# Attention of all four batches in halves of 256 queries with single-precision scores, in a fused attention and two-layer kernel

## The chip, the cores and the metric

One core of one Trainium2 chip. The metric is the device time of one execution in microseconds (us); less is better. The kernel before was run three times for its time, and one more execution was recorded by the hardware profiler.

## What is computed

Thresholded attention over 4 batches, 8 heads, 576 positions of 64 numbers, then two feed-forward layers over the 2304 rows that come out. All inputs are single precision.

```python
scores = scale * np.matmul(q, k.transpose(0, 1, 3, 2))       # 4, 8, 576, 576
thresh = np.max(scores, axis=-1, keepdims=True) - tau
scores = np.where(scores >= thresh, scores, -1000000000.0)
attn = np.exp(scores - np.max(scores, axis=-1, keepdims=True))
attn = attn / (np.sum(attn, axis=-1, keepdims=True) + 1e-09)
x = np.matmul(attn, v)                                       # to 2304 rows of 512
...
h = x @ w_in1; r = np.maximum(h, 0.0); x = (s * (r * r) + b) @ w_out1     # layer 1
h = x @ w_in2; x = (h * (1 / (1 + np.exp(-1.702 * h)))) @ w_out2          # layer 2
```

## The kernel before

**One planned order.** Every step is recorded with the engines it may run on, a cost and a due time (`Plan.add`). `Plan.run` then walks through the program once, always taking the ready step with the earliest due time, and writes out one fixed order for each engine. The due times come from the table `KN`. An engine executes its list strictly in order, so a step that has to wait holds up everything behind it on that engine.

**Attention** (`attention`, `heads`, `tile_step`). Two heads are handled together (`hp` 0 to 3), and the queries are cut in two parts: `w` = 0 holds queries 0 to 255, `w` = 1 queries 256 to 575. A pair (batch, `w`, `hp`) has four tiles of 128 queries (two per head), and with `w` = 1 a fifth that merges the last 64 queries of both heads. That makes 32 pairs and 144 tiles. For each tile TensorE writes scores into one of two buffers `S`; VectorE takes the negated row maximum `nm`; a bias `nb` and a bound `tb` are made from it; ScalarE takes the exponential `e`; and VectorE masks `e` by the bound, sums it, and with that lets go of `S`. For the units computed in half precision (all but the first two) ScalarE rounds `e` to `p16`, GpSimd computes the rest that the rounding left, a DMA transposes both into `PT`, and after the pair's last tile TensorE multiplies `PT` by V (the "mix").

`heads` decides the order of pairs by `KN["half"]`. Batches below it are "apart": all four head pairs of `w` = 0, then all four of `w` = 1, each with its own K and Q. With `half` = 2 this holds for batches 0 and 1. In batches 2 and 3 the two parts of a head pair follow each other and share K and Q (`"first"`).

The scores come in two forms, by `KN["parts"]` = 8. In batches 0 and 1 K is loaded as `kk` and scaled in place (L395), and single-precision products of 64 rows are used, each half of the array taking one half of the keys (L557). In batches 2 and 3 `prep_parts` cuts K and Q in two parts of reduced precision, one stacked above the other in 128 rows: ScalarE L411 and L419, VectorE L414 and L427, GpSimd L423 to clear borders. The scores are then four products of 128 rows per head and tile (L550).

**Layer 1** works on units of 256 rows: unit 2b + w needs the four pairs (b, w). `pair` makes the hidden values (L1035), `bank` the outputs (L1123). In `bank` one PSUM bank holds two halves of 256 columns. 48 products fill one half, ScalarE reads it with scale and bias (L1146), then 48 products fill the other half, which is read as well.

**Layer 2** works on blocks of 512 rows (`hidden7` L1333, `rows2` L1420).

**Engines.** TensorE, VectorE, ScalarE, GpSimd and SyncE, which issues every DMA, are PE, DVE, ACT, POOL and SP in the profile. A DMA whose buffer is not free yet holds up SP's whole queue.

Of the kernel before, what the change touches and what calls it, by code (L numbers as in the profile page):

```python
# [9 lines left out]
F32 = mybir.dt.float32  # L10
# [5 lines left out]
AF = mybir.ActivationFunctionType  # L16
ALU = mybir.AluOpType
# [4 lines left out]
P = 128  # L22
# [14 lines left out]
LOG_SP = 11.0 * math.log(2.0)  # L37
# [1 line left out]


KN = {
# [8 lines left out]
    "parts": 8, "raw": 1, "spread": 8,  # L50
}


# [219 lines left out]
def pe16(n, cols):  # L273
    return n * (cols * 0.4167 + 1.5)

def act(cols, psum=False):
    return cols * 0.834 + (53.0 if psum else 93.0)
# [12 lines left out]
class Kernel:  # L290
# [9 lines left out]
    def consts(self, pool):  # L300
        nc = self.nc
        self.ident = pool.tile([P, P], F32, name="ident")
        make_identity(nc, self.ident)
        self.ones = pool.tile([P, P], F32, name="ones")
        nc.vector.memset(self.ones, 1.0)
        self.turns, self.tw = 0, [Buf(None, "tw", None, None) for _ in range(KN["tw"])]
        for i, tw in enumerate(self.tw):
            tw.tile = pool.tile([P, 512, 2], F16, name="tw%d" % i)
            nc.vector.memset(tw.tile, 2.0 ** -24)
        sc = pool.tile([P, 3], F32, name="scal")  # L310
        for i, src in enumerate((self.tau, self.s, self.b)):
            nc.sync.dma_start(sc[:, i : i + 1], src.partition_broadcast(P))
        self.s_ap, self.b_ap = sc[:, 1:2], sc[:, 2:3]

        z = pool.tile([P, 1], F32, name="z")
        nc.vector.tensor_scalar(z, sc[:, 0:1], 0.0, None, ALU.is_ge)
        self.qs = pool.tile([P, 1], F32, name="qs")
        nc.vector.tensor_scalar(self.qs, z, 1.0 / math.sqrt(D), None, ALU.mult)
        t1 = pool.tile([P, 1], F32, name="t1")
        nc.vector.tensor_scalar(t1, z, -3e38, 3e38, ALU.mult, ALU.add)  # L320
        t2 = pool.tile([P, 1], F32, name="t2")
        nc.vector.tensor_scalar(t2, sc[:, 0:1], 0.0, None, ALU.max)
        self.under = pool.tile([P, 1], F32, name="under")
        nc.vector.tensor_tensor(self.under, t1, t2, ALU.add)


    def copy(self, dst, src, reads, writes, cols, scale=None, psum=False, also=0, **kw):
# [188 lines left out]
    def tile_step(self, p, i):  # L516


        nc, add = self.nc, self.plan.add
        k, q = p["k"], p["q"]  # L520
        Sp, swap = self.ps("S", [P, 2, 512]), []
        if not p["f32"] and p["unit"] * NP + p["hp"] < KN["sx"]:
# [3 lines left out]
            if self.nth % 3 == 0:  # L526
                Sp, swap = Buf(self.py, "Sx", [P, 2, 512], F32, 1), self.swaps
        T, q0 = p["T"], p["q0"]
        if i < 2 * T:
            h, t = divmod(i, T)  # L530
# [31 lines left out]
        else:  # L562
            used, cost = [k] + [q[h] for h, _ in heads], pe(1, HALF, True) + 200.0
        add({"PE": (cost, 60.0)}, scores, used + swap, [Sp])
        Sv = lambda: Sp[:, :, :HALF]
        nm = self.at("nm", [P, 1], F32, bufs=4)
        tb = self.at("tb", [P, 1], F32, bufs=4)
        pace, plain = p["pace"] / p["count"], p["f32"] and KN["nbs"]

        add(  # L570
            {"DVE": 668.0}, lambda _: nc.vector.tensor_reduce(nm.ap, Sv(), AX.XY, ALU.max, negate=True), [Sp], [nm],  # L571
            prio=self.plan.prio - KN["nm"] * pace,
        )
        add(
            {"POOL": 300.0} if p["f32"] and KN["tbp"] else {"DVE": 121.0},
            lambda e: self.eng[e].tensor_scalar(tb.ap, nm.ap, -1.0, self.under, ALU.mult, ALU.subtract), [nm], [tb],
            prio=self.plan.prio - KN["tb"] * pace,
        )
        nb = nm
        if not plain:  # L580
            nb = self.at("nb", [P, 1], F32, bufs=4)
            add(
                {"DVE": 65.0},
                lambda _: nc.vector.tensor_scalar(nb.ap, nm.ap, LOG_SP, None, ALU.add), [nm], [nb],  # L584
                prio=self.plan.prio - KN["tb"] * pace - 1.0,
            )
        e = self.at("e", [P, S], F32, bufs=KN["eb"])
        ev = lambda: e.ap.rearrange("p (a b) -> p a b", a=2)
        add(
            {"ACT": 624.0},  # L590
            lambda _: nc.scalar.activation(ev(), Sv(), AF.Exp, bias=nb.ap, scale=1.0), [Sp, nb], [e],  # L591
        )
        add(
            {"DVE": 735.0},
            lambda _: nc.vector.scalar_tensor_tensor(  # L595
                ev(), Sv(), tb.ap, ev(), ALU.is_ge, ALU.mult, accum_out=p["acc"][:, i, 0:1]
            ),
            [Sp, tb, e], [e, (p["acc"], i)], prio=self.plan.prio - KN["sc"] * pace,
        )
        if p["f32"]:  # L600
            Tp = Buf(self.px, "TP", [P, 2, 512], F32, 1)
# [290 lines left out]
    def gate(self, bank):  # L892

        return self.changes if bank.pool is self.pw else []
# [214 lines left out]
    def bank(self, u, ib):  # L1109

        nc, add, sv = self.nc, self.plan.add, self.scale_of(0)
        n = 256
        yp = self.bank_of([P, 2, n])
        ev = Buf(self.wp, "gt", [P, 2, n], F32, KN["gt"])
        terms = [(c, j, i, k) for c in range(NCH) for j in range(CH) for i, k in ((0, 0), (0, 1), (1, 0))]
        for h in range(2):
            i0 = 2 * ib + h
            m = KN["bn"]
            for part in range(0, 48, m):
                def mm(_, h=h, i0=i0, part=part):  # L1120
                    for t in range(part, part + m):
                        c, j, i, k = terms[t]
                        nc.tensor.matmul(  # L1123
                            yp[:, h, :], self.W[0, 1, c][:, i, j, i0 * P : (i0 + 1) * P], u["g"][c][:, k, j, :],
                            start=t == 0, stop=t == len(terms) - 1,
                        )
                c = part // 12
                add(
                    {"PE": (pe16(m, n), 60.0 * (part + m == 48))}, mm,
                    [self.W[0, 1, c], u["g"][c]] + self.gate(yp) + [(yp, 0)] * h, [(yp, h)],  # L1130
                )
            b = u["b"]
            if (ib, h) == (0, 0):
                ub = lambda: self.ub[:, b : b + 1]

                def scale(_):
                    if b == B:
                        nc.vector.tensor_reduce(ub(), self.ub[:, :B], AX.X, ALU.max)
                    y = sv["y"][:, b : b + 1]
                    nc.vector.tensor_scalar(y, ub(), ub(), sv["U"][:, 0:1], ALU.mult, ALU.mult)  # L1140
                    nc.vector.tensor_scalar(y, y, 2.0 ** 28, self.s_ap, ALU.mult, ALU.mult)
                if u["at"] == 0 or u["n"] == KN["fu"]:
                    add(self.tiny(2), scale, [sv["U"], (self.ub, b)], [(sv["y"], b)])
            add(
                {"ACT": act(n, True) + 190.0},
                lambda _, h=h, i0=i0: nc.scalar.activation(  # L1146
                    ev[:, h, :], yp[:, h, :], AF.Identity, bias=sv["b"][:, i0 : i0 + 1], scale=sv["y"][:, b : b + 1]
                ),
                [(yp, h), sv["b"], (sv["y"], b)], [(ev, h)],
            )  # L1150
        yd, cols = self.yd[u["b"]], slice(u["at"], u["at"] + n)
        self.load(
            lambda: yd[:, 2 * ib : 2 * ib + 2, cols], lambda: ev.ap, [(yd, (ib, u["at"]))], P * 2 * n * 4, reads=[ev]
        )
# [432 lines left out]
class Later:  # L1587


    pool = None  # L1590
# [50 lines left out]
```

## Time and profile before

| | us |
|---|---|
| median of 3 runs (lowest, highest) | 1044.27 (1041.58, 1047.13) |
| the profiled execution, its own time | 1043.83 |
| its span, first to last instruction | 1042.0 |
| TensorE busy | 986.9 |
| VectorE busy | 717.1 |
| ScalarE busy | 638.2 |
| GpSimd busy | 227.1 |

The profile is one execution on the hardware. Times inside it count from the start of the span. The granted clock is TensorE's, as a share of full speed. Idle time of an engine is put down to what ended it.

### The profile page before, as it was taken

To read this page: it belongs to the slowest core of one execution; us is meant where nothing else is said; L and a number is where in the kernel's file an instruction comes from. 1 tells how busy PE (TensorE), PEld (TensorE's weight loads), DVE (VectorE), ACT (ScalarE), POOL (GpSimd) and SP (SyncE) were. 2 spreads that over 40 slices of the span, in tenths; PEclk is the share of its full clock that TensorE was granted. 3 is DMA by queue.
4 is the path that set the end of the run, shared out by engine and by line. 5 is a ranking of instruction groups with operands and counts; after the bars stand their busy time and mean duration, and the time that the engine had idled before them with its cause. 6 is when DMAs were issued, how large, how long until landed. Compare 5 with 4: busy or idle time off the path is not lost.

```text
span 1042.0 us, 21397 instructions
## 1 busy us (share of the span) xinstructions
PE 986.9 (95%) x8181; PEld 747.5 (72%) x8181; DVE 717.1 (69%) x1670; ACT 638.2 (61%) x1220; POOL 227.1 (22%) x348
## 2 busy tenths in 40 slices
PE   5799989879999988999989999999999999999998
PEld 3466667658888876888868888887487487487483
DVE  6888897688888687987766867697257257256240
ACT  5787885588686675666755765685355355355241
POOL 1111134444544454444540000000001001000000
PEclk9999999899999998999989999999999999999999
DMA  7875589646678576566652336310010010000000
GB/s 250 279 268 168 161 170 222 130 89 152 127 163 184 127 155 127 130 129 136 147 102 84 114 112 214 120 51 3 31 51 2 31 50 2 31 31 1 31 11 20
DMA packets 170757, 114.80 MB, mean 110 GB/s; under 512 B 136280, under 2 KB 146592, under 8 KB 170656
## 3 DMA queue, kind: packets, MB, share of 16 engines
q1 hardware_dynamic: 170656, 113.45, 42.3%
q8 instruction: 64, 1.05, 0.4%
q14 instruction: 37, 0.30, 0.1%
HBM read 71.57 MB, written 10.00 MB: 78 GB/s over the span
## 4 chain that ended last, share of the span: by engine, by line
PE 53%; DVE 3%; DMA 3%; ACT 2%; issue 1%; POOL 0%; ACTq 0%; POOLq 0%; DVEq 0%
PE a L1420 18%; PE a L1333 8%; PE yy L1035 5%; PE y L1123 5%; PE yy L1123 4%; PE yy L1333 3%; PE y L1035 2%; PE d L1333 2%; PE S L550 2%; DMA PT<-p 2%; PE y L1333 2%; PE yy L1389 1%; PE T L690 1%; DMA wst<-in_moe_w_out 1%; PE y L1389 1%
## 5 line engine op out<-in xcount | busy, mean ns | idle before, releaser
L619 POOL TENSOR_TENSOR p<-e,p 128x512 f16<-128x512 f32 x108 | 129.9, 1203 | 187.5 <-ACT p L338 149.3
L1123 PEld LDWEIGHTS <-wb 128*128 128x128 f16 x1536 | 147.6, 98 | 26.5 <-issue 8.3
L1035 PEld LDWEIGHTS <-wb 128*128 128x128 f16 x1536 | 148.4, 98 | 25.1 <-issue 7.0
L1420 PE MATMUL a<-wb,g 128*128 128x512 f16 x648 | 144.4, 379 | 0.0
L1333 PEld LDWEIGHTS <-l 128*128 128x128 f16 x1344 | 131.5, 98 | 17.6
L595 DVE SCALAR_TENSOR_TENSOR e<-S,tb,e 128x576 f32<-128x576 f32 x144 | 116.0, 811 | 24.3 <-ACT e L591 21.9
L571 DVE TENSOR_REDUCE nm<-S 128x1 f32<-128x576 f32 x144 | 106.3, 750 | 36.1 <-PE S L557 19.4
L1420 PEld LDWEIGHTS <-g 128*128 128x128 f16 x648 | 63.4, 98 | 73.7
L1123 PE MATMUL yy<-g,wb 128*128 128x256 f16 x960 | 112.5, 273 | 2.6 <-ACT gt L1146 2.4
L591 ACT ACTIVATE e<-S,nb 128x576 f32<-128x576 f32 x108 | 78.8, 735 | 48.5 <-DVE nb L584 25.0
L1035 PE MATMUL yy<-xs,wb 128*128 128x256 f16 x912 | 107.5, 273 | 0.0
L1333 PE MATMUL a<-xs,l 128*128 128x256 f16 x768 | 95.6, 273 | 0.0
L338 ACT ACTIVATE p<-e 128x576 f16<-128x576 f32 x108 | 72.8, 677 | 24.9 <-DMA PT<-p 14.1
L1035 PE MATMUL y<-xs,wb 128*128 128x256 f16 x624 | 75.1, 273 | 4.5 <-ACT gt L1042 4.5
L340 ACT ACTIVATE gt<-a,x2y 128x512 f32<-128x512 f32 x18 | 12.4, 687 | 107.4 <-PE a L1420 84.3
L353 POOL TENSOR_TENSOR st<-wb 128x512 f32<-128x512 f32 x6 | 8.8, 1467 | 297.7 <-PE a L1333 171.6
L1123 PE MATMUL y<-g,wb 128*128 128x256 f16 x576 | 68.1, 273 | 2.0 <-ACT gt L1146 2.0
L1345 ACT ACTIVATE wb<-a 128x256 f32<-128x256 f32 x96 | 36.3, 378 | 33.0 <-PE a L1333 32.6
L1285 ACT ACTIVATE gt<-wb,x2h 128x256 f32<-128x256 f32 x64 | 36.5, 608 | 31.6 <-DVE wb L1352 31.6
L353 DVE TENSOR_TENSOR g<-gt,g 128x512 f16<-128x512 f32 x63 | 50.4, 801 | 7.6 <-ACT g L338 6.7
L550 PE MATMUL S<-kk,qb 128*128 128x288 f32 x160 | 41.2, 341 | 9.7 <-DVE nb L584 5.5
L1420 PE MATMUL a<-wb 128*128 128x512 f16 x216 | 49.4, 379 | 0.0
(194 smaller groups left out, 1749.6 us busy)
## 6 DMA issues: line engine op xcount, KB each, us to landing
wst<-in_moe_w_in SPq DMA_DIRECT2D x32, 512.0 KB, 5.4
wst<-in_moe_w_out SPq DMA_DIRECT2D x32, 512.0 KB, 4.1
rv<-in_v SPq DMA_DIRECT2D x32, 320.0 KB, 3.7
kk<-in_k SPq DMA_DIRECT2D x16, 288.0 KB, 4.6
raw<-in_k SPq DMA_DIRECT2D x16, 288.0 KB
yd<-gt SPq DMA_DIRECT2D x18, 256.0 KB, 2.5
raw<-in_q SPq DMA_DIRECT2D x16, 288.0 KB
wb<-yd SPq DMA_DIRECT2D x16, 256.0 KB, 4.3
```

The source lines that it names most:

```text
L338: nc.scalar.activation(dst(), src(), AF.Copy)
L353: engines, lambda e: self.eng[e].tensor_tensor(dst(), a(), b(), op), reads, writes, **kw
L550: nc.tensor.matmul(Sp[:, half, :HALF], q[h][j][:, qcols[h]], k[h][:, half * HALF : (half + 1) * HALF], start=(h, j) == (heads[0][0], 0), s ...
L571: {"DVE": 668.0}, lambda _: nc.vector.tensor_reduce(nm.ap, Sv(), AX.XY, ALU.max, negate=True), [Sp], [nm],
L591: lambda _: nc.scalar.activation(ev(), Sv(), AF.Exp, bias=nb.ap, scale=1.0), [Sp, nb], [e],
L595: lambda _: nc.vector.scalar_tensor_tensor(ev(), Sv(), tb.ap, ev(), ALU.is_ge, ALU.mult, accum_out=p["acc"][:, i, 0:1]),
L619: nc.gpsimd.tensor_tensor(p16[:, S + H2 :], e[:, :MAIN], p16[:, :MAIN], ALU.subtract)
L1035: nc.tensor.matmul(hps[:, h, :], W[:, i, j, kk * P : (kk + 1) * P], x[:, k, kk, :], start=t == 0, stop=t == len(terms) - 1,)
L1123: nc.tensor.matmul(yp[:, h, :], self.W[0, 1, c][:, i, j, i0 * P : (i0 + 1) * P], u["g"][c][:, k, j, :], start=t == 0, stop=t == len(terms) ...
L1285: lambda _, cols=cols, h=h: nc.scalar.activation(gt[:, cols], h(), AF.Tanh, scale=th[:, c : c + 1]),
L1333: nc.tensor.matmul(to(bank), W[:, u, m, j, kk * P : (kk + 1) * P], y[:, v, z, kk, :], start=n == 0 and not more, stop=n == 5, skip_group_c ...
L1420: nc.tensor.matmul(yp(), part(f, k), self.W[1, 1, f // CH][:, w, f % CH, :], start=n == 0, stop=n == 47,)
```

## The change

The diff, cut to its core. The table `KN` is replaced: the entries that select a form are shown, and nearly all due times in it have new values.

```diff
 KN = {
-    "first": 305.71, ... "half": 2, ... "t2": 670.54, "d2": 78.45, ... "tb": 54.91, ... "parts": 8,
+    "first": 278.77, ... "half": 4, "a2b": 247.09, "p2b": -5.0, "a3b": 450.05, "p3b": 4.03,
+    ... "t2": 642.87, "d2": 92.1, ... "tb": 13.38, ... "parts": 16,
 }
 # consts
+        self.signs, self.offs = pool.tile([P, 2], F32, name="signs"), pool.tile([P, 2], F32, name="offs")
+        nc.vector.memset(self.signs[:, 0:1], -1.0)
+        nc.vector.memset(self.signs[:, 1:2], 1.0)
+        nc.vector.tensor_scalar(self.offs[:, 0:1], self.under, -1.0, None, ALU.mult)
+        nc.vector.memset(self.offs[:, 1:2], LOG_SP)
 # tile_step
-        add(
-            {"POOL": 300.0} if p["f32"] and KN["tbp"] else {"DVE": 121.0},
-            lambda e: self.eng[e].tensor_scalar(tb.ap, nm.ap, -1.0, self.under, ALU.mult, ALU.subtract), [nm], [tb],
-        ...
-        if not plain:
-            add({"DVE": 65.0},
-                lambda _: nc.vector.tensor_scalar(nb.ap, nm.ap, LOG_SP, None, ALU.add), [nm], [nb], ...
+        both = self.at("tb", [P, 2], F32, bufs=4)
+        tb, nb = lambda: both[:, 0:1], lambda: both[:, 1:2]
+        if plain:
+            add({"POOL": 300.0},
+                lambda _: nc.gpsimd.tensor_scalar(tb(), nm.ap, -1.0, self.under, ALU.mult, ALU.subtract), [nm], [both], ...
+        else:
+            add({"DVE": 130.0},
+                lambda _: nc.vector.scalar_tensor_tensor(both.ap, self.signs, nm.ap, self.offs, ALU.mult, ALU.add), [nm], [both], ...
 # bank
                 if u["at"] == 0 or u["n"] == KN["fu"]:
                     add(self.tiny(2), scale, [sv["U"], (self.ub, b)], [(sv["y"], b)])
+        for h in range(2):
+            i0 = 2 * ib + h
             add(
                 {"ACT": act(n, True) + 190.0},
                 lambda _, h=h, i0=i0: nc.scalar.activation(
                     ev[:, h, :], yp[:, h, :], AF.Identity, bias=sv["b"][:, i0 : i0 + 1], scale=sv["y"][:, b : b + 1]
                 ),
-                [(yp, h), sv["b"], (sv["y"], b)], [(ev, h)],
+                [yp, sv["b"], (sv["y"], b)], [(ev, h)],
             )
```

So all four batches run "apart", `prep_parts` and the products of L550 are no longer used, one VectorE step writes bound and bias as two columns of one tile, and ScalarE reads a bank of layer 1 after both of its halves.

Counted over the whole program, VectorE has 128 instructions less (no `nb`, no L414 and L427), ScalarE 28, GpSimd 28; SP issues 16 DMAs more (16 more loads of `kk`, and 16 more each of `qa` and `qb`, against 32 loads of `raw` that go); TensorE has 160 products less, all of them scores. The new table also moves steps. Three places show how.

TensorE, the last pair of batch 3's attention (tiles 140 to 144 of 144), before; `S_7932` is the merged tile and the last two rows begin a mix:

```order
L550 MATMUL S_7887<-kk_7449,qb_7439 128x288 x2
L550 MATMUL S_7887<-kk_7449,qa_7437 128x288 x2
L550 MATMUL S_7907<-kk_7449,qb_7439 128x288 x2
L550 MATMUL S_7907<-kk_7449,qa_7437 128x288 x2
L638 MATMUL T_7919<-ident_71,ri_7912 4x128
L550 MATMUL S_7932<-kk_7449,qb_7439 128x288 x2
L550 MATMUL S_7932<-kk_7449,qa_7437 128x288 x2
L550 MATMUL S_7932<-kk_7699,qb_7557 128x288 x2
L550 MATMUL S_7932<-kk_7699,qa_7552 128x288 x2
L550 MATMUL S_7951<-kk_7699,qb_7557 128x288 x2
L690 LDWEIGHTS V_6334
L690 MATMUL T_7968<-PT0_7798,V_6334 64x256
```

Four of the five tiles stand behind each other with one small transpose among them, and no product of layer 1 stands between the first and the fifth.

The same engine and place in the changed kernel, from the second of the five tiles (`S_7361` is the merged one):

```order
L562 MATMUL S_7353<-kk_6917,qa_6860 128x288 x2
L562 MATMUL S_7361<-kk_6917,qa_6860 64x288 x2
L562 MATMUL S_7361<-kk_6917,qb_6927 64x288 x2
L644 MATMUL T_7368<-ident_71,ri_7356 5x128
L1129 LDWEIGHTS wb_2755
L1129 MATMUL y_7303<-g_7131,wb_2755 128x256
```

Behind the merged tile come 30 products of layer 1, and between the first and the fifth tile there are 72.

VectorE, tiles 106 and 107 (the end of batch 2), before; `kk_5681` is the preparation of a coming pair's K:

```order
L571 TENSOR_REDUCE nm_5685<-S_5668 128x1
L414 SCALAR_TENSOR_TENSOR kk_5681<-raw_5515,qs_88,kk_5681 64x576
L584 TENSOR_SCALAR nb_5701<-nm_5685 128x1
L576 TENSOR_SCALAR tb_5703<-nm_5685,under_94 128x1
L571 TENSOR_REDUCE nm_5705<-S_5689 128x1
L584 TENSOR_SCALAR nb_5712<-nm_5705 128x1
L576 TENSOR_SCALAR tb_5714<-nm_5705,under_94 128x1
L595 SCALAR_TENSOR_TENSOR e_5707,acc_5471<-S_5668,tb_5703,e_5707 128x576
```

The preparation of K stands between a tile's maximum and the bias that its exponential waits for.

The same engine and tiles in the changed kernel:

```order
L575 TENSOR_REDUCE nm_5327<-S_5316 128x1
L589 SCALAR_TENSOR_TENSOR tb_5341<-signs_96,nm_5327,offs_97 128x2
L601 SCALAR_TENSOR_TENSOR e_5337,acc_4959<-S_5273,tb_5312,e_5337 128x576
L575 TENSOR_REDUCE nm_5375<-S_5363 128x1
L589 SCALAR_TENSOR_TENSOR tb_5387<-signs_96,nm_5375,offs_97 128x2
L601 SCALAR_TENSOR_TENSOR e_5377,acc_4959<-S_5316,tb_5341,e_5377 128x576
```

One step of two columns follows each maximum, and the preparation of K is gone from this engine.

ScalarE, the first bank of layer 1 behind the attention, before (`y_8187` is the bank, `l16` are weights of layer 2 being rounded):

```order
L1146 ACTIVATE gt_8312<-y_8187,b0_3211,y0_2634 128x256
L340 ACTIVATE l16_8342<-wb_2997,s1_8157 128x512 x4
L340 ACTIVATE l16_8342<-st_8350,s1_8157 128x512
L340 ACTIVATE l16_8342<-st_8340,s1_8157 128x512
L1146 ACTIVATE gt_8312<-y_8187,b0_3211,y0_2634 128x256
```

The two reads of the bank stand apart, one behind each half.

The same engine and place in the changed kernel:

```order
L345 ACTIVATE l16_7862<-wb_3059,s1_7698 128x512 x4
L345 ACTIVATE l16_7862<-st_7870,s1_7698 128x512
L345 ACTIVATE l16_7862<-st_7860,s1_7698 128x512
L1154 ACTIVATE gt_7926<-y_7721,b0_3148,y0_2660 128x256 x2
L345 ACTIVATE l16_7862<-wb_3059,s1_7698 128x512 x2
```

Both reads now stand together.

## Rows read from the trace of the kernel before

**Rows 1.** The page, section 1: busy time, share of the span, instructions.

```profile
PE 986.9 (95%) x8181; PEld 747.5 (72%) x8181; DVE 717.1 (69%) x1670; ACT 638.2 (61%) x1220; POOL 227.1 (22%) x348
```

**Rows 2.** Busy time by stretch: length, then each engine, clock, DMA share, GB/s.

```profile
182.00:234.00 52.00, 43.16 (x398) 31.62 (x397) 39.84 (x104) 35.79 (x65) 22.08 (x30) 0.93 0.52 109
234.00:364.00 130.00, 129.39 (x1411) 111.14 (x1410) 107.06 (x267) 93.39 (x171) 60.52 (x88) 1.00 0.71 151
364.00:416.00 52.00, 43.96 (x407) 36.97 (x407) 40.27 (x96) 34.40 (x58) 26.10 (x38) 0.90 0.70 141
416.00:520.00 104.00, 102.28 (x1042) 89.74 (x1039) 83.22 (x213) 71.59 (x126) 53.66 (x80) 1.00 0.63 134
520.00:546.00 26.00, 20.95 (x198) 17.61 (x195) 16.76 (x47) 13.76 (x24) 11.21 (x16) 0.87 0.53 106
702.00:1037.00 335.00, 335.00 (x2227) 217.75 (x2224) 159.62 (x338) 143.12 (x304) 8.01 (x6) 1.00 0.07 23
```

**Rows 3.** TensorE's timeline, 395 to 416: start, length, instruction, idle time before it.

```profile
395.83 0.82 PE L550 MATMUL S<-kk,qb 128*128 128x288 f32 x2 [3.14 <-DVE e L595]
...
397.06 3.20 PE L690 MATMUL T<-PT,V 128*64 128x256 f16 x28
...
415.43 1.69 PE L690 MATMUL T<-PT,V 128*64 128x256 f16 x27 [1.80 <-DMA PT<-p]
```

**Rows 4.** TensorE's timeline, 525 to 531: the tiles of batch 3's last pair.

```profile
527.95 0.82 PE L550 MATMUL S<-kk,qb 128*128 128x288 f32 x2 [1.68 <-DVE nb L584]
...
530.92 0.82 PE L550 MATMUL S<-kk,qb 128*128 128x288 f32 x2 [1.46 <-DVE nb L584]
```

**Rows 5.** VectorE's timeline, 392 to 394: what stands ahead of a bias.

```profile
392.01 1.67 DVE L414 SCALAR_TENSOR_TENSOR kk<-raw,qs,kk 64x576 fp32r<-64x576 f32 x1
393.71 0.15 DVE L584 TENSOR_SCALAR nb<-nm 128x1 f32<-128x1 f32 x1
```

**Rows 6.** TensorE's timeline: score tiles of both forms and what follows each.

```profile
181.39 0.76 PE L557 MATMUL S<-kk,qa 64*128 64x288 f32 x4
182.08 0.41 PE L659 MATMUL T<-ident,ri 128*64 128x128 f32 x2
182.41 0.46 PE L557 MATMUL S<-kk,qa 64*64 64x288 f32 x2
...
183.06 1.99 PE L1094 MATMUL y<-g,wb 128*128 128x256 f32 x8
...
288.97 0.51 PE L550 MATMUL S<-kk,qb 128*128 128x288 f32 x2
...
290.11 1.48 PE L1123 MATMUL yy<-g,wb 128*128 128x256 f16 x12
...
295.60 0.51 PE L550 MATMUL S<-kk,qb 128*128 128x288 f32 x2
...
296.21 0.83 PE L1123 MATMUL yy<-g,wb 128*128 128x256 f16 x6
```

**Rows 7.** VectorE's groups by form: count, busy us, mean ns, idle before them.

```profile
L576 DVE TENSOR_SCALAR tb<-nm,under 128x1 f32<-128x1 f32 x108 | 21.5, 202 | 0.0
...
L584 DVE TENSOR_SCALAR nb<-nm 128x1 f32<-128x1 f32 x108 | 15.6, 145 | 0.9
L414 DVE SCALAR_TENSOR_TENSOR kk<-raw,qs,kk 64x576 fp32r<-64x576 f32 x16 | 15.1, 944 | 0.5
...
L427 DVE TENSOR_TENSOR qa<-raw,qb 128x576 fp32r<-128x576 f32 x16 | 13.3, 831 | 9.2 <-ACT qb L419 9.2
```

**Rows 8.** Layer 1's output products: who TensorE waited for, then two stretches.

```profile
  ACT gt L1146: 4.4, 7
...
601.22 4.75 PE L1123 MATMUL y<-g,wb 128*128 128x256 f16 x42 [0.65 <-ACT gt L1146]
605.80 4.75 PE L1035 MATMUL yy<-xs,wb 128*128 128x256 f16 x42
```

**Rows 9.** Waits of SP's queue (us, times, longest), and for K's scaling (L395).

```profile
SPq L357 <- DVE wb L836: 81.3, 45, 11.9
...
  PE S L557: 8.1, 1
```

More of the change, by code (lines that the diff above doesn't have):

```diff
@@ L41 @@
 KN = {
[8 rows of a table removed]
-    "parts": 8, "raw": 1, "spread": 8,
[9 rows of a table added]
 }
@@ L566, in tile_step @@
         nm = self.at("nm", [P, 1], F32, bufs=4)
-        tb = self.at("tb", [P, 1], F32, bufs=4)
         pace, plain = p["pace"] / p["count"], p["f32"] and KN["nbs"]
@@ L573, in tile_step @@
         )
-        add(
-            {"POOL": 300.0} if p["f32"] and KN["tbp"] else {"DVE": 121.0},
-            lambda e: self.eng[e].tensor_scalar(tb.ap, nm.ap, -1.0, self.under, ALU.mult, ALU.subtract), [nm], [tb],
-            prio=self.plan.prio - KN["tb"] * pace,
-        )
-        nb = nm
-        if not plain:
-            nb = self.at("nb", [P, 1], F32, bufs=4)
-            add(
-                {"DVE": 65.0},
-                lambda _: nc.vector.tensor_scalar(nb.ap, nm.ap, LOG_SP, None, ALU.add), [nm], [nb],
-                prio=self.plan.prio - KN["tb"] * pace - 1.0,
-            )
+        both = self.at("tb", [P, 2], F32, bufs=4)
+        tb, nb = lambda: both[:, 0:1], lambda: both[:, 1:2]
+        if plain:
+            add(
+                {"POOL": 300.0},
+                lambda _: nc.gpsimd.tensor_scalar(tb(), nm.ap, -1.0, self.under, ALU.mult, ALU.subtract), [nm], [both],
+                prio=self.plan.prio - KN["tb"] * pace,
+            )
+        else:
+            add(
+                {"DVE": 130.0},
+                lambda _: nc.vector.scalar_tensor_tensor(both.ap, self.signs, nm.ap, self.offs, ALU.mult, ALU.add), [nm], [both],
+                prio=self.plan.prio - KN["tb"] * pace,
+            )
+        biased = nm if plain else both
         e = self.at("e", [P, S], F32, bufs=KN["eb"])
@@ L590, in tile_step @@
             {"ACT": 624.0},
-            lambda _: nc.scalar.activation(ev(), Sv(), AF.Exp, bias=nb.ap, scale=1.0), [Sp, nb], [e],
+            lambda _: nc.scalar.activation(ev(), Sv(), AF.Exp, bias=nm.ap if plain else nb(), scale=1.0), [Sp, biased], [e],
         )
@@ L595, in tile_step @@
             lambda _: nc.vector.scalar_tensor_tensor(
-                ev(), Sv(), tb.ap, ev(), ALU.is_ge, ALU.mult, accum_out=p["acc"][:, i, 0:1]
+                ev(), Sv(), tb(), ev(), ALU.is_ge, ALU.mult, accum_out=p["acc"][:, i, 0:1]
             ),
-            [Sp, tb, e], [e, (p["acc"], i)], prio=self.plan.prio - KN["sc"] * pace,
+            [Sp, both, e], [e, (p["acc"], i)], prio=self.plan.prio - KN["sc"] * pace,
         )
```

17 rows, old and new, of the table KN are left out of this document.

## The prediction

> **What bounds the kernel.** I read the page first: TensorE is busy for 986.9 of 1042.0 us, VectorE for 717.1 [rows 1]. So the time is TensorE's work plus TensorE's losses, and a change on another engine counts only where TensorE waits for that engine. Next I read busy time by stretch, to see where the losses lie [rows 2]. From 702 to 1037, in layer 2, TensorE is busy for 335.00 of 335 us: nothing can be gained there except by less work. From 234 to 364 it idles for 0.6 us in 130. But in 364 to 416 it idles for 52 - 43.96 = 8.0 us, in 416 to 520 for 1.7, in 520 to 546 for 5.1, and before that, in 182 to 234, for 8.8. In three of these the granted clock is below 1 as well: 0.93, 0.90 and 0.87.
>
> TensorE's own timeline then says what the waits are. In 364 to 416 the longest are 3.14 us for VectorE's masking to let go of a score buffer, and 1.80 us for a transposing DMA that came late [rows 3]. In 520 to 546 single tiles of scores come 3 us apart, each held up by VectorE for 1.46 or 1.68 us [rows 4]. The order rows above say why just there: these tiles stand one behind another, with none of layer 1's products between them. VectorE's timeline shows the same spot from the other side: its preparation of K took 1.67 us and stood between a maximum and the bias that the exponential needs [rows 5].
>
> **The change part by part.** The sum is made against the profiled execution: 1043.8 us, of which the span is 1042.0. The median of the runs, 1044.3, is 0.05% above it. This measurement can tell about 0.5%, 5 us, from no change.
>
> *Scores.* 64 plain tiles and 8 merged ones change their form. A plain tile in single precision takes 0.69 us from its start to the next instruction (181.39 to 182.08), one in parts 0.61 (295.60 to 296.21); a merged tile takes 0.65 (182.41 to 183.06) against 1.14 (288.97 to 290.11) [rows 6]. That is 64 x 0.08 = +5.1 and 8 x -0.49 = -3.9, together **+1.2 us**. All of it is TensorE's own work and lies on the path. Bounds: -3.9 if plain tiles cost the same, +5.1 if merged ones do. On this the Trainium skill speaks against the change: "FP8 and Floating Point Precision", section "TensorE Precision Notes", says that true FP32 takes four passes through the array. Counted that way a tile would be eight passes and the sum higher by the price of the third rival; the measured 0.69 fits another of its pages, "TensorE: Matmul & The Clock Gate", part 3, which lets products in different row groups run together.
>
> *Preparation.* VectorE loses L414 and L427, 16 x 0.944 + 16 x 0.831 = 28.4 us, and for 108 tiles two steps of 0.145 and 0.202 become one [rows 7]. No row shows a step with two columns and a pointer: it lies between 0.145 (one column) and 0.347 (both); I take 0.20, the longer of the two it replaces. That is another 108 x 0.147 = 15.9 us. Both lie beside TensorE's work, so by themselves they count zero; they matter through the next term.
>
> *Where the tiles stand.* In the last pair of batch 3 the first and the fifth tile now have 72 products of layer 1 between them. Such a product takes 4.58 / 42 = 0.109 us (601.22 to 605.80) [rows 8], so that is 7.9 us of cover where there was none; VectorE's pace in the burst was one tile per 3 us [rows 4], 12 us for four steps. With the tiles themselves TensorE now has 7.9 + 5 x 0.69 = 11.4 us of work there, and VectorE has less to do per tile. At the end of batch 2 the new order behaves alike (144 products between tiles 104 and 111, where before the first one came behind tile 110). So I count the idle time of 364 to 546 as gone: 8.0 + 1.7 + 5.1 = 14.8, less 0.65 of it that is a bank wait and comes below: **-14.2 us**. What is late next are small waits as in 234 to 364, 0.6 per 130 us; over these 182 us **+0.9**. Bounds: none of it gained, or all.
>
> *The clock.* With the waits goes the lower of TensorE's two levels, half speed. A clock of 0.90 over 52 us means 10.4 us at the lower level, 0.87 over 26 means 6.8 [rows 2]; of these TensorE spent 3.1 us waiting in the first case [rows 3], and 1.46 and some 0.9 of the 1.68 us in the second [rows 4]. The rest ran at half speed: (7.3 + 4.4) / 2 = **-5.8 us**. A mix shows it directly: 3.20 us at 397, after the long wait, against 1.69 at 415 [rows 3].
>
> *Bank reads.* In layer 1 the second half of a bank cannot start before ScalarE has read the first half: seven waits, 4.4 us, 0.65 the typical one [rows 8]. With both reads behind both halves nothing is between the halves: **-4.4 us**. In return a bank comes free one read later. I count nothing for that, because banks rotate over three buffers with the hidden values' products between; without that cover it costs 0.65 for each of 16 banks, 10 us.
>
> *Loads.* SP issues 16 DMAs more, and K is loaded and scaled anew for each of the 16 pairs of batches 2 and 3. In batches 0 and 1 that is so already, and TensorE waited for K's scaling once, at the very start [rows 9]: zero, with the price in the second rival. The early stretch to 234 keeps its tiles, forms and waits; zero, though VectorE's shorter bias step could give some of the 8.8 us back.
>
> The sum: 1043.8 + 1.2 - 14.2 + 0.9 - 5.8 - 4.4 = **1021.5 us**, 22 us or 2.1% less.
>
> **The rivals.** *Bursts come back elsewhere.* The new order still has places where two tiles stand together, and real durations differ from the planned ones. If half of the waits and of the clock loss stay: 1021.5 + (14.2 + 5.8) / 2 = 1031.5. For it: 182 to 234 shows waits without such a burst. Against: 234 to 364, where tiles and products alternate as they now do throughout, has 0.6 us in 130. If all of them stay, because VectorE's total and not its order makes them, only the bank reads and the scores count: 1043.8 + 1.2 - 4.4 = 1040.6, within 0.5% of before.
>
> *K comes late (slower).* Every pair of batches 2 and 3 now needs its own K at its first tile, and these loads stand in SP's queue, which was held up by weight staging 45 times for 81.3 us, 1.8 us each [rows 9]. If each of the 16 loads comes 1.8 us late and TensorE waits: 1021.5 + 28.8 = 1050.3. It decides from 22 / 16 = 1.4 us per load. Against it: the loads are issued during the pair before, and in batches 0 and 1 the same queue cost nothing after the first.
>
> *Scores by passes (slower).* One product of 288 columns in reduced precision takes 1.14 / 8 = 0.14 us [rows 6]. Four passes for each of a tile's two products are 8 x 0.14 = 1.14 us instead of 0.61: 64 x 0.53 = 34 us more, less the 5.1 counted: 1050. This is what the rule of the skill's precision page would come to. The rows of batches 0 and 1 show 0.69, so it would need something that only batches 2 and 3 have.
>
> **How the numbers follow.** The forecast gets 0.70, bursts by half 0.13, all waits staying 0.06, late K 0.08, passes 0.03. Faster by over 0.5% means under 1039: 0.70 + 0.13 = 0.83, less a little for the bursts' upper end, **0.82**. Within 0.5%: 0.06 and that little, **0.07**. Slower: **0.11**. The range goes down to 1012, where the early stretch gives back all 8.8 us, and up to 1040, short of late K and passes.
>
> **What would show it.** In the changed profile: TensorE idle under 2 us in the last 150 us of attention, and a clock of 1.00 there; no wait of TensorE for layer 1's bank reads; score tiles of batches 2 and 3 at 0.69; a two-column step near 0.2 us; VectorE near 717 - 44 = 673 us busy. Layer 2 stays a solid 335 us and starts 22 us earlier. I am wrong if TensorE waits for K at the starts of pairs, if tiles in batches 2 and 3 take over 0.8 us, or if waits for masking of over 1 us appear after 234.

## The result, and the profile after

The changed kernel takes **1028.4 us** (median of 4 runs, 1026.3 to 1028.7) against 1043.7 before (4 runs, 1041.6 to 1047.1): ratio 0.9846, 95% interval 0.9816 to 0.9876. The forecast was 1021.5 with a range of 1012 to 1040: the direction and the range hold, the gain is 15 us instead of 22. The profiled execution took 1028.6 us, 1.8 of it outside its span, so the spans can be compared: 1042.0 before, 1026.8 now.

The page's first section, which answers to [rows 1]:

```profile
span 1026.8 us, 21127 instructions
PE 990.0 (96%) x8181; PEld 719.8 (70%) x8181; DVE 698.7 (68%) x1542; ACT 619.2 (60%) x1192; POOL 211.9 (21%) x320
```

The span fell by 15.2 us, though TensorE's busy time rose by 3.1. TensorE's count is the same as before although it has 160 products less, because the profile shows a single-precision product as two records (the two products of a tile are x4 in [rows 6]). Busy time by stretch of the changed kernel (columns as in [rows 2]), the first two stretches of before behind it:

```profile
0.00:52.00 52.00, 36.16 (x201) 20.73 (x202) 39.32 (x88) 33.47 (x64) 8.06 (x26) 0.93 0.75 262
52.00:104.00 52.00, 47.84 (x343) 30.94 (x342) 45.55 (x110) 42.25 (x86) 6.70 (x19) 0.97 0.74 249
...
182.00:234.00 52.00, 47.16 (x436) 35.39 (x432) 41.23 (x97) 35.04 (x62) 21.08 (x31) 1.00 0.67 130
234.00:364.00 130.00, 127.74 (x1340) 97.52 (x1339) 104.57 (x231) 90.45 (x166) 56.86 (x82) 0.99 0.73 165
364.00:416.00 52.00, 51.23 (x514) 38.32 (x513) 35.74 (x80) 33.51 (x56) 24.23 (x35) 1.00 0.69 136
416.00:520.00 104.00, 101.89 (x1006) 77.26 (x1004) 82.39 (x188) 66.52 (x116) 49.95 (x69) 1.00 0.69 141
520.00:546.00 26.00, 26.00 (x304) 21.98 (x303) 11.69 (x32) 11.05 (x21) 7.96 (x11) 1.00 0.47 95
687.00:1022.00 335.00, 335.00 (x2225) 217.65 (x2223) 161.47 (x346) 145.47 (x309) 10.69 (x7) 1.00 0.07 25
```

```profile
0.00:52.00 52.00, 35.55 (x208) 21.20 (x210) 40.02 (x85) 34.33 (x66) 8.50 (x26) 0.97 0.77 265
52.00:104.00 52.00, 49.59 (x370) 32.82 (x366) 44.49 (x108) 43.50 (x88) 7.78 (x22) 1.00 0.66 219
```

From 364 to 546 TensorE idles for 0.8 + 2.1 + 0 = 2.9 us where it idled for 14.8 [rows 2], and the clock is 1.00 where it was 0.90 and 0.87. Layer 2 is the same solid 335 us, 15 us earlier. In the first 104 us the clock is lower than before.

A span splits into TensorE's idle time (span less busy), the loss at the lower clock level, and TensorE's work at full clock (the rest). The lower level is half speed (a granted clock of 0.50), so the loss is half of the time for which TensorE was busy at it. Three of the stretches at that level before (columns as in [rows 2]):

```profile
0.00:21.80 21.80, 11.19 (x41) 6.54 (x42) 13.26 (x29) 10.92 (x18) 3.11 (x14) 1.00 0.75 265
390.40:400.60 10.20, 6.87 (x42) 5.12 (x42) 8.35 (x18) 5.18 (x9) 5.82 (x10) 0.50 0.53 102
527.00:533.80 6.80, 4.39 (x17) 3.91 (x17) 4.32 (x15) 2.90 (x5) 3.44 (x6) 0.50 0.51 100
```

The view shows 1.00 for the first stretch only because the trace's record of the clock begins at its end. The tiles tell otherwise (TensorE's timeline of before):

```profile
13.67 1.33 PE L557 MATMUL S<-kk,qb 64*128 64x288 f32 x4
14.93 1.33 PE L606 MATMUL TP<-ident,e 128*128 128x128 f32 x5
```

A tile takes 1.26 us from start to start here (13.67 to 14.93) and 0.69 at 181 us [rows 6]. So the time up to the first record (21.8 us before, 22.2 now) is counted at the lower level too. TensorE was busy at it for 31.6 us in all before and for 28.0 now. The loss is an estimate: the tile takes 1.83 times as long and not 2, by which the loss would be up to 1.5 us smaller and the work as much larger.

| profiled run | span | idle | lower clock | work |
|---|---|---|---|---|
| before | 1042.0 | 55.1 | 15.8 | 971.1 |
| after | 1026.8 | 36.8 | 14.0 | 976.0 |
| difference | -15.2 | -18.3 | -1.8 | +4.9 |
| by the prediction | -22.3 | -17.7 | -5.8 | +1.2 |

The idle time fell in sum as forecast. What is missing is 3.7 us of work and 4.0 us of clock. The four largest waits of TensorE that are left (us, times, longest):

```profile
PE S L562 <- ACT kk L400: 8.1, 1, 8.1
PE TP L612 <- DVE e L601: 7.9, 5, 3.0
PE S L562 <- DVE e L601: 3.6, 11, 0.5
PE y L1041 <- ACT gt L1048: 3.4, 3, 1.4
```

No wait for a bank's read stands in the whole list any more [rows 8], and K is waited for once, at the start, as before [rows 9].

### The profile page after: what moved, and what is told of

Same layout as the page of the kernel before. It is cut to its first block, busy times and chain, and to the rows that moved or that the text cites. A ratio compares the mean times of both kernels' runs of the same rounds, so it can differ in the third digit from the quotient of the medians.

```text
span 1026.8 us, 21127 instructions
## 1 busy us (share of the span) xinstructions
PE 990.0 (96%) x8181; PEld 719.8 (70%) x8181; DVE 698.7 (68%) x1542; ACT 619.2 (60%) x1192; POOL 211.9 (21%) x320
## 4 chain that ended last, share of the span: by engine, by line
PE 79%; DVE 9%; ACT 6%; DMA 3%; issue 2%; SPq 1%; POOL 0%; ACTq 0%; DVEq 0%
PE a L1428 18%; PE yy L1041 8%; PE a L1341 8%; PE yy L1129 8%; PE S L562 7%; PE y L1041 5%; PE y L1129 5%; PE T L696 4%; PE yy L1341 3%; DVE e L601 2%; PE y L1100 2%; PE d L1341 2%; DVE nm L575 2%; PE y L1341 2%; PE TP L612 2%
## 5 line engine op out<-in xcount | busy, mean ns | idle before, releaser
L625 POOL TENSOR_TENSOR p<-e,p 128x512 f16<-128x512 f32 x108 | 126.9, 1175 | 202.6 <-ACT p L343 169.1
L1341 PEld LDWEIGHTS <-l 128*128 128x128 f16 x1344 | 131.5, 98 | 17.6
L575 DVE TENSOR_REDUCE nm<-S 128x1 f32<-128x576 f32 x144 | 106.4, 751 | 38.2 <-PE S L562 38.1
L1041 PE MATMUL yy<-xs,wb 128*128 128x256 f16 x936 | 111.4, 273 | 0.0
L597 ACT ACTIVATE e<-S,tb 128x576 f32<-128x576 f32 x108 | 78.7, 734 | 50.2 <-POOL p L626 23.1
L1129 PE MATMUL yy<-g,wb 128*128 128x256 f16 x864 | 103.2, 274 | 0.0
L1129 PE MATMUL y<-g,wb 128*128 128x256 f16 x672 | 79.3, 273 | 0.0
L1041 PE MATMUL y<-xs,wb 128*128 128x256 f16 x600 | 72.5, 273 | 3.5 <-ACT gt L1048 3.4
L562 PE MATMUL S<-kk,qa 64*128 64x288 f32 (+1 forms) x320 | 62.3, 473 | 12.3 <-ACT kk L400 8.1
L358 POOL TENSOR_TENSOR st<-wb 128x512 f32<-128x512 f32 x7 | 11.1, 1584 | 288.3 <-DVE wb L358 113.0
L562 PE MATMUL S<-kk,qb 64*128 64x288 f32 (+1 forms) x320 | 60.8, 460 | 1.1 <-DVE e L601 1.0
```

Of the source, the lines that this page charges most:

```text
L358: engines, lambda e: self.eng[e].tensor_tensor(dst(), a(), b(), op), reads, writes, **kw
L562: nc.tensor.matmul(Sp[to, half, :HALF], q[h][r, qcols[h]], k[r, h * HALF : (h + 1) * HALF])
L597: lambda _: nc.scalar.activation(ev(), Sv(), AF.Exp, bias=nm.ap if plain else nb(), scale=1.0), [Sp, biased], [e],
L625: nc.gpsimd.tensor_tensor(p16[:, S + H2 :], e[:, :MAIN], p16[:, :MAIN], ALU.subtract)
L1041: nc.tensor.matmul(hps[:, h, :], W[:, i, j, kk * P : (kk + 1) * P], x[:, k, kk, :], start=t == 0, stop=t == len(terms) - 1,)
L1129: nc.tensor.matmul(yp[:, h, :], self.W[0, 1, c][:, i, j, i0 * P : (i0 + 1) * P], u["g"][c][:, k, j, :], start=t == 0, stop=t == len(terms) ...
```

## The experiments

**Theory.** The waits went because VectorE's preparation went and the score tiles now stand apart; the bank reads give their 4 us; the missing gain is a price that single-precision tiles put on the product ahead of them. **Rivals:** the shorter bias step or the halves made the gain; the extra work has another source.

### Each part alone

bank_alone is the kernel before with the changed bank reads; step_alone with the two-column step; form_alone with this line; order_alone with the whole table of numbers of the changed kernel.

```diff
-    "parts": 8, "raw": 1, "spread": 8,
+    "parts": 16, "raw": 1, "spread": 8,
```

> The kernel before, with only the reads of layer 1's banks put behind both halves. By the prediction's term the bank waits (4.4 us in the trace of before) go and nothing takes their place: 1043.7 - 4.4 = about 1039.3 us, ratio 0.996, and no wait of TensorE on layer 1's second halves for ScalarE. Rival: the order is planned anew and the waits only move to the next late thing: 1043.7 us, ratio 1.000.

> The kernel before, with only bias and bound of a tile made in one two-column step. If VectorE's work lies beside TensorE's, as the prediction counted it: 1043.7 us within 2 us, ratio 0.998 to 1.002, and the two-column step takes about 0.20 us. Rival: VectorE's total makes the waits of 364 to 546 us, and a shorter chain per tile takes half of them away with their clock: (14.8 + 5.8) / 2 = 10 us less, about 1033 us, ratio 0.990.

> The kernel before, with only the form of the scores changed: single precision in batches 2 and 3 too, pairs of 512 queries and all other numbers as before; 64 plain and 8 merged tiles change, 28.4 us of preparation leave VectorE. The prediction's term alone gives 1043.7 + 1.2 = 1044.9 us if the bursts stay. Theory from the trace of after: a product ahead of a single-precision tile is about 0.18 us longer than one ahead of a tile in parts, some 64 x 0.18 = 11.5 us in all, so about 1055 us less what the lighter VectorE gives back, 1046 to 1055, with TensorE's busy time up by 5 us or more. Rival: VectorE's preparation made the waits, so without it idle time and clock come back: 1044.9 - 14.2 - 5.8 = about 1025 us.

> The code of the kernel before with all the table's numbers of the changed kernel: halves of 256 queries, the due times and the form of the scores as after, but the bias and the bound in two steps and the bank reads per half. If table and form bring what is left beside the bank reads, as the prediction has it: 1028.4 + 4.4 = about 1032.8 us, ratio to before 0.990. Rival: the changed code matters more than that (VectorE's longer chain per tile brings the bursts back): 1038 us or more.

| run | median us | ratio to before, 95% | idle | lower clock | work |
|---|---|---|---|---|---|
| bank_alone | 1049.1 | 1.0034, 1.0011 to 1.0056 | 57.3 | 21.9 | 968.7 |
| step_alone | 1059.2 | 1.0118, 1.0087 to 1.0150 | 65.9 | 17.6 | 974.8 |
| form_alone | 1037.9 | 0.9923, 0.9896 to 0.9951 | 48.3 | 9.6 | 980.2 |
| order_alone | 1034.8 | 0.9893, 0.9866 to 0.9919 | 43.4 | 11.3 | 978.9 |

Two expectations failed outright: bank_alone and step_alone are slower. The bank waits are gone in bank_alone, but the planner has made a new order around the edit, and in it the mixing product waits for a transposing DMA (TensorE's timeline of bank_alone):

```profile
520.40 3.15 PE L690 MATMUL T<-PT,V 128*64 128x256 f16 x27 [6.10 <-DMA PT<-p]
```

So an edit and a new order were measured together. The next section takes them apart.

order_alone came near its expectation. form_alone lies between theory and rival: work is 9 us up (980.2 against 971.1), though TensorE's busy time rose by 2.9 and not by the 5 or more of the theory, and the bursts are gone all the same. Its stretches of 364 to 546:

```profile
364.00:416.00 52.00, 50.82 (x484) 38.14 (x482) 35.41 (x95) 31.45 (x53) 21.52 (x32) 1.00 0.68 129
416.00:520.00 104.00, 103.59 (x1039) 77.58 (x1038) 83.02 (x225) 67.88 (x119) 48.32 (x70) 1.00 0.68 127
520.00:546.00 26.00, 25.34 (x274) 21.49 (x272) 9.56 (x29) 11.59 (x20) 7.29 (x11) 1.00 0.40 82
```

That is 2.3 us of idle time at a clock of 1.00, with the pairs of batches 2 and 3 in the sequence of before and with its due times. So the form, with the order that the planner makes for it, removes the bursts; the halves are not needed for it. The order of TensorE's instructions shows it too. Of the 83 score tiles from the 62nd on, so many directly follow the tile before them, without a product of layer 1 between: 31 before, 29 in bank_alone and step_alone, 8 in form_alone, 5 in order_alone, 14 after. The crowding goes with the tiles in parts, whose K and Q have to be split first; which of the planner's rules makes it was not tried. Nor does a run separate the new order from VectorE's lighter load. At the last pair of before the bursts came without the preparation: VectorE's last step of the preparation starts at 519.09 us, and at 528 and 531 TensorE still waited for a bias for 1.68 and 1.46 us [rows 4].

From form_alone to order_alone (halves and due times) 3 us are gained, little more than the runs' spread, and from there to after (step and bank reads) 6.4, each with a new order; 4.8 us of order_alone's idle time are waits for bank reads (2.8 and 2.0 in its list of waits).

### The two small edits with the order held

Here the planner sees the kernel before, so that TensorE's instructions stand in the same order as before; only what a step issues is changed. In bank_same_order the first read of a bank is issued with the second:

```diff
-                lambda _, h=h, i0=i0: nc.scalar.activation(
-                    ev[:, h, :], yp[:, h, :], AF.Identity, ...
+                lambda _, h=h, i0=i0: [
+                    nc.scalar.activation(ev[:, j, :], yp[:, j, :], AF.Identity, ...) for j in (0, 1) if h == 1
+                ],
```

In step_same_order the bias step makes both columns, in twice as many buffers, and the bound's step issues nothing:

```diff
-                lambda _: nc.vector.tensor_scalar(nb.ap, nm.ap, LOG_SP, None, ALU.add), [nm], [nb],
+                lambda _: nc.vector.scalar_tensor_tensor(nb.ap, self.signs, nm.ap, self.offs, ALU.mult, ALU.add), [nm], [nb],
```

> The kernel before, planned as before so that every other instruction keeps its place, but the read of a bank's first half is issued with the read of its second half. Theory (the term holds, and bank_alone lost its gain to a new order): the seven bank waits go, 4.4 us: about 1039.5 us, ratio 0.996. Rival (banks come free later and TensorE then waits for a bank): 1044 us or more, with waits of layer 1's first halves on ScalarE.

> The kernel before, planned as before so that every other instruction keeps its place, but VectorE's bias step makes bias and bound in two columns and the bound's own step is left away. Theory of the prediction (VectorE's steps lie beside TensorE's work): 1044 us within 2. Rival (the chain from maximum to exponential is what the bursts wait for: 5.5 us of waits of score tiles for the bias): the waits shrink by a third to a half with some of the clock, 1039 to 1042 us. If step_alone's loss of 12 us came from the step itself and not from the new order, this run is slower too: 1056 us.

bank_same_order: 1041.4 us, ratio **0.9964** (0.9943 to 0.9984), 3.8 us less by the ratio and 2.7 by the medians (1044.1 for before); no wait for a bank read is left in its list. Its profiled execution, one of its slower ones (1044.1), does not show the gain: idle time is 54.3 us against 55.1, because waits for masking grew. step_same_order: 1045.5 us, ratio **1.0016** (0.9997 to 1.0035), no gain. Both terms agree with the runs as they were counted, 4.4 and 0. So the losses of bank_alone and step_alone come with their new orders, not from the edits.

step_same_order also shows why the step gives VectorE nothing. The two-column step in the changed kernel's view of line L589 (minimum, median and maximum in ns, first and last start in us):

```profile
L589 DVE SCALAR_TENSOR_TENSOR tb<-signs,nm,offs x108: 180/220/1174, 120.5 to 523.8; 128x2 f32<-128x2 f32 x108
```

The median of 0.22 us is near what I took (0.20). But it costs 38.1 us for 108 steps, 0.363 each, where the two old steps cost 21.5 + 15.6 = 37.1 [rows 7]. The long ones stand beside GpSimd's subtraction. The changed kernel's timelines at 263 us, first GpSimd's, then VectorE's:

```profile
263.40 1.15 POOL L625 TENSOR_TENSOR p<-e,p 128x512 f16<-128x512 f32 x1 [1.49 <-ACT p L343]
```

```profile
263.45 1.12 DVE L589 SCALAR_TENSOR_TENSOR tb<-signs,nm,offs 128x2 f32<-128x2 f32 x1
...
265.35 0.20 DVE L589 SCALAR_TENSOR_TENSOR tb<-signs,nm,offs 128x2 f32<-128x2 f32 x1
```

Of the 108 steps, the 56 that began with no such subtraction under way took 0.21 us on average, 0.22 at most; the 52 others took 0.52, up to 1.17. The old steps read one tile each and took the same either way (0.20 and 0.14). The Trainium skill has the rule, in "SBUF — State Buffer", section "Who interferes with whom": a VectorE instruction with two SBUF inputs contends with a GpSimd instruction that reads SBUF, and one with at most one SBUF input, outside the two-port modes, does not. The trace agrees. The same explains the 1.67 us of K's preparation in [rows 5]: GpSimd's subtraction ran from 391.90 to 393.06. Of the 16 steps of L414, the 12 that began with no subtraction under way took 0.82 us, the 4 others 0.91 to 1.72.

### The price of a single-precision tile

In the next four runs each tile is computed twice, with one extra full-array 16-bit product either ahead of both or between them. The products are the same in both runs of a couple; the order of all steps is that of after (single) or before (parts).

```diff
+        def scores(_):
+            one = self.ident[:, :].bitcast(F16)
+            full = lambda: nc.tensor.matmul(Sp[:, 0, :256], one[:, :P], one, start=True, stop=True)
+            again = not p["f32"]
+            for step in (once, full, once) if again else (once,):
+                step()
```

This is single_apart. The together runs have `(full, once, once)`, and the parts runs do the same with the tiles in parts.

> The changed kernel, same order of all steps, but each of the 108 score tiles behind the first batch's plain part is computed twice, with one extra full-array product of 256 columns ahead of both: full, tile, tile. It is the base of the next run and has the same number of products. By the rows (0.11 + 0.69 us a tile, at most) 108 x 0.80 = 86 us more than after at most: 1028 + 86 = up to 1115 us; less if two tiles in a row overlap.

> The same as the run single_together, with the same products, but the extra full-array product between the two tiles: tile, full, tile. So there is one more change from full-array products to a single-precision row tile, and one more back, in each of the 108 tiles, and nothing else. Theory (each entry into a single-precision tile costs about 0.18 us): 108 x 0.18 = 19 us more than single_together. Rival (no price for the change; the longer products before a tile come from elsewhere): the same time within 3 us.

> The kernel before, same order of all steps, but each of the 72 score tiles in parts (batches 2 and 3) is computed twice with one extra full-array product of 256 columns ahead of both: full, tile, tile. Base of the next run. By the rows 64 x (0.61 + 0.11) + 8 x (1.14 + 0.11) = 56 us more than before: about 1100 us.

> The same as the run parts_together, with the extra full-array product between the two tiles: tile, full, tile. A tile in parts uses the full array, as the product does, so by the theory that the price is for the change of the array's tiling there is none to pay here: the same time as parts_together within 3 us. Rival (any change between 16-bit and 32-bit products costs 0.18 us): 72 x 0.18 = 13 us more.

| run | median us | lowest to highest |
|---|---|---|
| single_together | 1086.7 | 1085.3 to 1087.5 |
| single_apart | 1115.8 | 1111.4 to 1116.2 |
| parts_together | 1086.9 | 1084.4 to 1089.2 |
| parts_apart | 1088.2 | 1086.1 to 1094.9 |

Both bases came out at 1087 us, where up to 1115 and about 1100 were expected. single_apart is 29.1 us slower than single_together: **29.1 / 108 = 0.27 us** for each extra change to a single-precision row tile and back. In parts the same rearrangement costs 1.4 / 72 = 0.02 us, within the runs' spread. So the theory holds, with a price of 0.27 rather than 0.18, and it isn't a price of 32-bit data as such: parts are 32-bit products of the full array too. Where it lies (TensorE's timelines of single_together, single_apart, parts_together):

```profile
297.38 2.14 PE L1048 MATMUL y<-xs,wb 128*128 128x256 f16 x18
299.35 0.27 PE L566 MATMUL S<-ident 128*128 128x256 f16 x1
299.56 1.24 PE L562 MATMUL S<-kk,qa 64*128 64x288 f32 x8
300.73 0.72 PE L1136 MATMUL yy<-g,wb 128*128 128x256 f16 x5
```

```profile
299.48 3.44 PE L1048 MATMUL yy<-xs,wb 128*128 128x256 f16 x30
302.84 0.76 PE L562 MATMUL S<-kk,qb 64*128 64x288 f32 x4
303.53 0.28 PE L566 MATMUL S<-ident 128*128 128x256 f16 x1
303.75 0.76 PE L562 MATMUL S<-kk,qb 64*128 64x288 f32 x4
304.43 0.83 PE L1048 MATMUL yy<-xs,wb 128*128 128x256 f16 x6
```

```profile
301.12 0.27 PE L561 MATMUL S<-ident 128*128 128x256 f16 x1
301.15 0.51 PE L550 MATMUL S<-kk,qb 128*128 128x288 f32 x2
```

From start to start, the 16-bit product takes 0.21 us ahead of a row tile (299.35 to 299.56) and 0.03 ahead of a tile in parts; among its like it takes 0.109. And two row tiles together take 1.17 us (299.56 to 300.73), one alone 0.69 (302.84 to 303.53), so that the second of two costs only 0.48. Within the 1.17 us the first half of the first tile takes 0.35 and the last half of the second 0.34, the two halves between them 0.24 each. One pays when the array goes into row tiles, about 0.1 us in the product ahead and 0.1 in the first half, and 0.1 again when it comes out: 0.30 by the rows, near the 0.27 of the measured times.

Parts are products in reduced precision, so these runs alone leave a rival open: the price could be that of full single precision. Two other places of the traces speak for the tiling. In the changed kernel the 16-bit product ahead of a 16-bit mixing product, which uses 64 of the array's columns, takes 0.203 us too (25 places), without any 32-bit data. And in the kernel before, layer 1's full-array single-precision product takes 0.309 us ahead of a row tile (8 places) and 0.216 ahead of its like, though all of them are single precision.

The Trainium skill states the mechanism: by "TensorEngine Tiling (Array Packing)", section "Key Properties", a change of the tiling mode drains TensorE. The rows agree. It gives no price; these runs do.

The kernels themselves show the same. Over 234 to 560, without waits (medians from the timeline): a row tile alone takes 0.69 and the 16-bit product of layer 1 ahead of it 0.09 too long; a tile in parts takes 0.62 and the product ahead of it 0.08 too short.

### A version with fewer changes of tiling

If the price is per change, two tiles of a head should stand together. In pairs they are one step of the plan:

```diff
+        two = not p["f32"] and i in (0, T) and not twin
+        Sn = p["twin"] = self.ps("S", [P, 2, 512]) if two else None
...
+            if two:
+                for half in range(2):
+                    r, c = slice(half * H2, (half + 1) * H2), slice(at + P, at + 2 * P)
+                    nc.tensor.matmul(Sn[:, half, :HALF], q[h][r, c], k[r, h * HALF : (h + 1) * HALF])
...
-        add({"PE": (cost, 60.0)}, scores, used + swap, [Sp])
+        if not twin:
+            add({"PE": (cost * (1 + two), 60.0)}, scores, used + swap, [Sp] + [Sn] * two)
```

> The changed kernel with the two score tiles of a head issued directly one behind the other, in one step of the plan, so that TensorE enters the single-precision form once for both: 48 such pairs, of which some 18 stood together already. If each entry and exit costs the 0.27 us that single_apart against single_together shows, 30 x 0.27 = 8 us less than the changed kernel: about 1020 us, if layer 1's products between the pairs cover VectorE's work on both tiles. Rival (two tiles at once fill both score buffers, so that each pair waits for VectorE's mask of the one before): 1030 to 1045 us.

It took 1042.4 us, ratio 0.9985 (0.9972 to 0.9998): slower than the changed kernel, in the rival's range but not by its mechanism. TensorE's busy time fell to 982.7, 7.3 us less than after (8 expected), and the score tiles waited for masks for 0.4 us, against 3.6 in after. But idle time rose by 21.2 us (58.0), most of it one wait (timeline of pairs):

```profile
578.13 0.59 PE L873 MATMUL yy<-fro,ones 128*128 128x4 f32 x2 [14.44 <-ACT sq L859]
```

It is the norm of layer 2's weights, which were not staged yet. The attention's last mixing product ends at 561 us in this order and at 544 in the changed kernel, and SP issued no load of weights from 561 to 572; which link of that chain was late first was not tried. pairs_planned tells the planner the measured cost of a tile, and has due times that were searched anew with the planner (24 numbers of the table, among them the start of layer 2's weights, w2, 335.44 to 351.97):

```diff
-            add({"PE": (cost * (1 + two), 60.0)}, scores, used + swap, [Sp] + [Sn] * two)
+            add({"PE": (cost + 100.0 + 500.0 * two, 60.0)}, scores, used + swap, [Sp] + [Sn] * two)
```

> The run pairs with the planner told what the traces show of a tile (0.78 us for one, 1.28 us for two in one step, the longer product ahead of it included) and with due times searched anew, so that layer 2's weights are staged before TensorE reaches their norm. Theory: the 14.4 us wait of pairs goes and its gain in TensorE's work stays (busy 982.7 against 990.0 us of the changed kernel): 1028.4 - 7.3 = about 1021 us, or 1042.4 - 14.4 = 1028 us at least, ratio to before 0.978 to 0.985, and no wait for the norm over 2 us. Rival (the wait only moves, since the attention ends later when tiles come in pairs): 1035 us or more with another wait of TensorE of over 5 us between 520 and 700 us.

**1021.2 us** (median of 6, 1018.8 to 1023.2), ratio to before **0.9764** (0.9739 to 0.9789). It beats both kernels, and of the wait for the norm 0.3 us are left. First its page, then its stretch from 546 to 690:

```profile
span 1021.4 us, 21139 instructions
PE 976.3 (96%) x8181; PEld 724.0 (71%) x8181; DVE 693.1 (68%) x1539; ACT 620.0 (61%) x1192; POOL 218.9 (21%) x323
```

```profile
546.00:690.00 144.00, 142.91 (x1346) 127.67 (x1344) 117.69 (x235) 109.53 (x223) 9.66 (x6) 1.00 0.35 122
```

By the same split (TensorE's record of the clock begins at 28.2 us here) work is 966.7 us, 9.3 less than after, the lower clock takes 4.4 less (9.6), and idle time is 8.3 more (45.1). pairs, with the due times of after, has the same work within 1.5 us (965.3), so the lower work goes with the pairing. What of the clock and the idle time is due to the new due times isn't told apart by this one run.

## Why the prediction was right, and where it was off

- **Scores** (+1.2): the mis-sized term. TensorE's work rose by 4.9 us, and by 9.1 and 7.8 in form_alone and order_alone, where fewer tiles stand together (8 and 5 instead of 14). The step "a plain tile in single precision takes 0.69 us from its start to the next instruction, one in parts 0.61" read both durations rightly, but left out the product ahead, which a row tile lengthens and a tile in parts shortens. Summed from start to start without waits, and with half of the time at the lower clock level taken off, layer 1's 16-bit products went from 339.4 to 345.5 us (+6.1); the tiles themselves went from 96.0 to 95.3. The rule on draining stands in the Trainium skill's page on tiling ("TensorEngine Tiling (Array Packing)", section "Key Properties"). It speaks against this change, and I weighed another page in its place. The third rival, a tile as eight passes one behind another, is refuted: 0.69 us in all batches.
- **Where the tiles stand** (-14.2 + 0.9): right in size. Idle time from 364 to 546 fell by 11.9 us; 182 to 234 gave back another 4.0, which the range held open but the sum did not count, so that the sum of the idle time came out partly by luck. And the cause is the form of the scores, with the preparation and the order that go with it, by form_alone; the halves don't matter for it. Which of the preparation and the order it is stays open in 364 to 416; at batch 3's last pair it was not the preparation.
- **The clock** (-5.8): right where it was counted. From 364 to 546 TensorE had been busy at the lower level for 6.87 + 4.39 us, half of which is 5.6, and now it is at full clock there throughout. But the total fell only by 1.8, because the lower level came in elsewhere: 3.4 us more loss in the first 104 us (10.6 against 7.2) and 1.7 from 234 to 364, with 1.2 less between. The order doesn't set the first 104 us alone: the five traces with TensorE's order of before (before, bank_same_order, step_same_order and the two parts runs) lose 4.5 to 8.6 us there, the three with the order of after (after and the two single runs) 7.9 to 10.6. What else decides it stays open.
- **Bank reads** (-4.4): confirmed with the order held, -3.8 by the ratio (1.7 to 6.0).
- **Preparation** (0 on the path): right for the two-column step, which gains nothing with the order held; the rest was not tried alone. For VectorE's total it was wrong: 698.7 us instead of 673, mostly because the two-column step saves nothing.
- **Loads** (0): right; K is waited for once.
- Of the rivals, "bursts come back" comes nearest in time, but not by its mechanism: no burst is left after 234, and the longest wait there is 1.5 us. Of the signs, VectorE's total failed, and narrowly TensorE's idle time in the last 150 us of attention: 2.7 us (394 to 544) instead of under 2.

## What to carry to other kernels

Price a change of an operation's form by what it does to its neighbours too: on TensorE the start-to-start time of the product ahead of it belongs to the cost, and row tiles are cheaper in groups. Where a planner sets the order, an edit tried alone is measured together with a new order; hold the order, or both signs can come out. And cheaper work pays only if what comes after it is ready: pairs gave its 7 us of TensorE's busy time back in one wait for weights.

## What was unexpected of the hardware

- Going from full-array products to row tiles of 64 and back costs TensorE 0.27 us, about a third of it each in the product ahead, in the first and in the last half of the tiles; going from 16-bit to full-array products in parts and back costs 0.02.
- A VectorE step of two columns that reads two tiles took 0.21 us alone and up to 1.17 us beside GpSimd's subtraction; the two one-input steps that it replaced took 0.20 and 0.14 either way.
